# Two of six block inversions done over 16-token blocks, with their joins on TensorE, and a new order of the first batch

## The chip, the cores and the metric

The kernel runs on one core of a Trainium2 chip, in float32 throughout. The metric is the device time of one execution in microseconds (us), the median of several runs. Five engines have queues of their own and work through them in order: TensorE (PE, matrix products; its weight loads are listed apart as PEld), VectorE (DVE), ScalarE (ACT), GpSimd (POOL) and SyncE (SP), which here only issues transfers. TensorE writes to PSUM, eight banks of 128x512 float32; the other engines copy from there to SBUF.

## What is computed

The first half is a delta-rule attention over 4 batches, 8 heads, 768 tokens and head width 48; the second half mixes the result with a two-dimensional Fourier transform and a two-layer network:

```python
for t in range(S):                                    # per batch and head, state D x D
    y[t] = q[t] @ state
    state = state + beta[t] * outer(k_n[t], v[t] - state.T @ k_n[t])
u  = x + real(fft(fft(x, axis=1), axis=2))            # x: y as (batch, 768, 384)
un = (u - mean(u)) / sqrt(var(u) + 1e-6)
out = u + relu(un @ w_ch1) @ w_ch2                    # 384 -> 1536 -> 384
```

`k_n` is `k` over its norm. The two weight matrices come as float64 and are turned into float32 on the core.

## The kernel before

**Tiling of the attention.** Tokens are handled in chunks of 64. A *group* (index `g`, 24 in all, 6 per batch, `NL` = 6) is 128 tokens, two chunks, of all 8 heads. Within a chunk the recurrence becomes a triangular system: with G the products of the keys among themselves, the inverse of a unit lower triangular matrix is needed for each head and chunk. The kernel inverts blocks of 32 tokens (`W` = 32) and joins two of them to a chunk of 64 by two small products (in `pre_m`). Four groups make a *round* (`RL` = 4, index `r`, 6 rounds): their 128 partitions x 32 blocks are inverted together.

**The parts of the work**, each a generator that stops at its `yield`s, so that a schedule can advance several of them in turn:

- `pre_a(g)`: transposes the keys (4 products with the identity, tile `one` from `C`), copies them to `KT` on ScalarE, then 32 products `KT` x `KT` into `pair`, copied out to `G` (what is inverted) and `GX` (what joins two blocks). It also issues the load of a later group's keys into the buffer just read (`load_c(g + 3)`; three buffers `C`).
- `invert(r)`: all on VectorE: a transposition of the 1024 columns (L304), some 14 small operations for the norms, then forward substitution in 31 steps of two operations (L345 multiply into `tmp`, L349 add into `M`), and two transpositions (L352, L353). 
- `pre_q(g)`: the same for the queries: `QT`, and `LQ`, the masked products of keys and queries.
- `pre_m(g)`: scales the values (POOL L398), spreads the inverses (POOL L402), joins the two 32-blocks with two sets of 16 products and the copies L415 and L426, and makes `WT` and `U0` with 32 products.
- `step(g, c)`: the recurrence proper, one chunk: products S x WT, subtraction from U (L462), products U x K, addition to S (L481); after the second chunk of a group the outputs: S x QT and U x LQ into `pair`, copied and added (L502, L511) into `x`.
- `fourier(b)`: three folds of `x` (POOL L528 and L529, then six VectorE operations L532 to L539, each fold of token blocks t and t + 3), products with the tables `evt` and `odt` (`pf`), copies to `F`, and per 128 tokens the products with `dtab` (`pb`), additions and the statistics for the normalization.
- `mlp(b)`: three times 19 pieces: transposes of the normalized rows, 12 pieces of first-layer products (`ph`, into `hT`), 6 pieces of second-layer products (`po`).
- `weights()`: float64 to float32 in 12 pieces, six of w_ch1 and six of w_ch2, each a chain ScalarE (L231), VectorE (L232, L234, L237), ScalarE (L239), VectorE (L241, L243), POOL (L246). A piece uses the scratch of the piece before it, so one piece ends before the next is written. The pieces of w_ch2 use a scratch (tag `O`) that `fourier(0)` uses too.

**The order.** Inside `with tc.manual_schedule(...)` the order is written out by hand: first the keys of rounds 0 and 1, the inversions `inv0` and `inv1` in alternation on VectorE, the queries of batch 0, then `pre_m(0)` and the twelve steps of batch 0, with pieces of `inv1`, of the weights and of the folds put between them. After the block, batches 1 to 3 are interleaved: while the steps of batch b + 1 run, `mlp(b)` is spread beside them by `beside(n)`, with the keys and the inversion of the next round. There a scheduler places the instructions, and it also moves work from behind the block into gaps of it.

**What waits for what**, as far as the change touches it: `pre_m(g)` needs the round's inverse; `step(g, 0)` needs `pre_m(g)`; the folds need all six groups of a batch; `pf` needs the folds; the w_ch2 conversion needs `pf` to be done with its scratch; `po` needs w_ch2; `pre_m(8)` needs the inverse of round 2. Transfers that SyncE issues wait in SyncE's order for their buffers to come free. All PSUM tiles share pools of two buffers (`one`, `pair`, and `post` for everything after the attention).

## Time and profile before

| | us |
|---|---|
| three runs | 822.41, 826.55, 833.77 (median 826.55) |
| the profiled execution | 822.35 |
| its span, first to last instruction | 820.4 |
| first transposition of round 0's inversion starts | 15.64 |
| first product that reads round 0's inverse | 61.78 |
| first U x K product (`step(0, 0)`) | 69.27 |
| output of batch 0's last group added (L511) | 153.48 |
| last fold of batch 0 ends | 161.3 |
| last `pf` product of batch 0 ends | 174.2 |
| last weight piece: POOL starts | 236.32 |
| first product that reads round 2's inverse | 261.10 |

Busy times over the span: PE 706.0 (86%), VectorE 410.9 (50%), ScalarE 203.9, POOL 132.0. A profile line of a group reads: source line, engine, operation, output tile <- input tiles, shapes, count | busy us, mean ns of one | idle us just before them, and what ended that idle time. A line of the timeline reads: start, duration, engine, the same names, and in brackets the idle time before it. A float32 product appears as two records, so 32 products are `x64`; a transposition is one record. "PEclk" is the TensorE clock granted by its throttle, in tenths of full speed. Nearly all products are issued by one helper, so they all carry line L104 (L107 for transposes) and are told apart by their tiles.

### The profile page before, as it was taken

How to read it: one execution, taken by the hardware profiler on the slowest of the kernel's cores; microseconds unless marked ns; L12 is line 12 of the kernel's file. 1: busy time of each engine (PE TensorE's matmuls, PEld its weight loads, DVE VectorE, ACT ScalarE, POOL GpSimd, SP SyncE). 2: the span in 40 equal slices, each digit the busy share in tenths (PEclk: the TensorE clock that was granted, in tenths of full speed). 3: DMA queues.
4: the chain of work that ended last, by engine and by line, in shares of the span. 5: the costliest groups of instructions: out<-in, count | busy, mean ns of one | idle time of the engine just before them, and what ended most of it. 6: DMA issues, size and time to landing. Idle time of an engine off the chain costs nothing.

```text
span 820.4 us, 23216 instructions
## 1 busy us (share of the span) xinstructions
PE 706.0 (86%) x10344; PEld 543.3 (66%) x10344; DVE 410.9 (50%) x1004; ACT 203.9 (25%) x470; POOL 132.0 (16%) x150
## 2 busy tenths in 40 slices
PE   6537565398888999899998998899999999899998
PEld 4427464387656867568866767777768677686774
DVE  2897756546997118946258515698222141511110
ACT  4312333163321322124321223212223111210010
POOL 6231135302311101131100102102000020100000
PEclk8555555596998899999998999999999999899999
DMA  9821134323300321112121122002010000000000
GB/s 133 209 44 29 29 106 110 92 41 88 112 16 21 61 54 33 35 30 40 37 46 30 21 46 46 12 10 45 16 46 17 11 12 1 19 1 20 10 10 19
DMA packets 107382, 36.06 MB, mean 44 GB/s; under 512 B 99633, under 2 KB 102930, under 8 KB 107282
## 3 DMA queue, kind: packets, MB, share of 16 engines
q1 hardware_dynamic: 105586, 33.50, 18.3%
q8 instruction: 81, 1.33, 0.7%
q0 software_dynamic: 512, 0.79, 0.6%
q10 hardware_dynamic: 1184, 0.30, 0.3%
q14 instruction: 19, 0.16, 0.1%
HBM read 29.84 MB, written 4.72 MB: 42 GB/s over the span
## 4 chain that ended last, share of the span: by engine, by line
PE 55%; DVE 28%; issue 5%; POOL 5%; DMA 3%; ACT 3%; SPq 1%; ACTq 0%; POOLq 0%; DVEq 0%
PE po L104 17%; PE ph L104 17%; PE pair L104 8%; DVE M L349 5%; DVE tmp L345 5%; PE one L104 5%; PE pf L104 3%; DMA C<-in_k_dram 3%; PE one L107 2%; PE pb L104 2%; POOL w L246 1%; DVE A L304 1%; DVE A L352 1%; DVE G L353 1%; PE ptr L107 1%
## 5 line engine op out<-in xcount | busy, mean ns | idle before, releaser
L104 PE MATMUL ph<-unT,w 128*128 128x256 f32 x864 | 211.1, 399 | 9.5 <-DVE hT L619 5.9
L104 PE MATMUL po<-w,hT 128*128 128x384 f32 x576 | 198.1, 496 | 5.9 <-POOL w L246 3.2
L104 PEld LDWEIGHTS ph<-unT,w 128*128 128x128 f32 x864 | 166.0, 198 | 37.8 <-DVE hT L619 8.8
L104 PEld LDWEIGHTS po<-w,hT 128*128 128x128 f32 x576 | 108.4, 193 | 74.1 <-POOL w L246 3.3
L619 DVE TENSOR_SCALAR hT<-ph 128x256 f32<-128x256 f32 x72 | 30.3, 421 | 112.6 <-PE ph L104 112.6
L349 DVE TENSOR_TENSOR M<-M,tmp 128x135 f32<-128x135 f32 (+15 forms) x186 | 70.8, 382 | 4.8
L345 DVE TENSOR_TENSOR tmp<-A,M 128x60 f32<-128x60 f32 (+15 forms) x186 | 67.4, 364 | 4.4
L617 ACT ACTIVATE hT<-ph 128x256 f32<-128x256 f32 x72 | 27.5, 382 | 145.6 <-PE ph L104 142.5
L629 DVE TENSOR_TENSOR x<-x,po 128x384 f32<-128x384 f32 x24 | 13.2, 552 | 97.4 <-PE po L104 97.4
L104 PE MATMUL one<-V,MT 64*64 64x48 f32 x768 | 48.6, 245 | 0.9 <-ACT MT L426 0.8
L402 POOL TENSOR_TENSOR MT<-A,pack 128x512 f32<-128x512 f32 x24 | 26.1, 1096 | 136.2 <-PE one L104 85.3
L104 PEld LDWEIGHTS one<-V,MT 64*64 64x64 f32 x768 | 44.3, 163 | 2.8 <-ACT MT L426 1.7
L398 POOL TENSOR_TENSOR V<-V,nT 128x384 f32<-128x384 f32 x24 | 20.7, 863 | 154.5 <-DMA V<-in_v_dram 90.8
L104 PE MATMUL pair<-MT,K 64*64 64x64 f32 x768 | 43.5, 260 | 1.6 <-ACT MT L426 1.0
L104 PEld LDWEIGHTS pair<-MT,K 64*64 64x64 f32 x768 | 39.4, 154 | 3.5 <-issue 2.1
L104 PE MATMUL pair<-S,WT 48*64 48x48 f32 x704 | 22.9, 247 | 21.8 <-DVE S L481 17.5
L104 PEld LDWEIGHTS pair<-S,WT 48*64 48x64 f32 x704 | 17.1, 153 | 31.2 <-DVE S L481 18.6
L104 PEld LDWEIGHTS pair<-U,K 64*64 64x64 f32 x704 | 17.1, 153 | 29.1 <-DVE U L462 14.3
L104 PE MATMUL pair<-U,K 64*64 64x48 f32 x704 | 23.5, 248 | 14.4 <-DVE U L462 12.6
L104 PE MATMUL one<-G,GX 32*32 32x32 f32 x768 | 19.8, 207 | 14.9 <-DVE G L353 14.9
L481 DVE TENSOR_TENSOR S<-S,pair 128x192 f32<-128x192 f32 x40 | 14.0, 350 | 37.0 <-PE pair L104 36.9
L415 ACT ACTIVATE XM<-one 32x256 f32<-32x256 f32 x48 | 18.0, 375 | 54.9 <-PE one L104 53.8
(111 smaller groups left out, 928.6 us busy)
## 6 DMA issues: line engine op xcount, KB each, us to landing
w<-in_moe_w_ch_dram SPq DMA_DIRECT2D x12, 768.0 KB
Q<-in_q_dram SPq DMA_DIRECT2D x24, 192.0 KB
out_dram<-x SPq DMA_DIRECT2D x24, 192.0 KB
C<-in_k_dram SPq DMA_DIRECT2D x23, 192.0 KB
K<-in_k_dram SPq DMA_DIRECT2D x88, 48.0 KB
V<-in_v_dram SPq DMA_DIRECT2D x88, 48.0 KB
evt<-k_even SPq DMA_DIRECT2D x1, 579.0 KB
odt<-k_odd SPq DMA_DIRECT2D x1, 576.0 KB
```

The source lines that it names most:

```text
L104: nc.tensor.matmul(o, lhsT=lhsT, rhs=rhs, start=start, stop=stop, skip_group_check=True)
L107: nc.tensor.matmul(o, lhsT=src, rhs=ident[0:src.shape[0], 0:src.shape[0]], is_transpose=True, start=start, stop=True, skip_group_check=True)
L246: nc.gpsimd.tensor_tensor(dst, man.rearrange("p (c f) -> p c f", c=c), num.bitcast(F32).rearrange("p (c f) -> p c f", c=c), op=ALU.mult)
L345: nc.vector.tensor_tensor(t, A[:, j + 1:W, j:j + 1].broadcast_to([128, n, j + 1]), M[:, j:j + 1, 0:j + 1].broadcast_to([128, n, j + 1]), o ...
L349: nc.vector.tensor_tensor(M[:, j + 1:W, 0:j + 1], M[:, j + 1:W, 0:j + 1], t, op=ALU.add)
L398: nc.gpsimd.tensor_tensor(V.rearrange("p c j d -> p (c j) d"), V.rearrange("p c j d -> p (c j) d"), nT[:, m8, None].broadcast_to([128, 8, ...
L402: nc.gpsimd.tensor_tensor(MT, MTd[:, m8, None, :].broadcast_to([128, 8, 2, W]), m_blk[:, None, :, None].broadcast_to([128, 8, 2, W]), op=A ...
L415: nc.scalar.activation(XM[rw].rearrange("p m s -> p (m s)"), px[rw, 0:8 * W], ACT.Copy, scale=-1.0)
L481: nc.vector.tensor_tensor(s1v, s0.rearrange("p h j e -> p h (j e)"), pk, op=ALU.add)
L617: nc.scalar.activation(hT[:, fc, :], ph, ACT.Relu)
L619: nc.vector.tensor_scalar(hT[:, fc, :], ph, 0.0, None, op0=ALU.max)
L629: nc.vector.tensor_tensor(x[:, T, :], x[:, T, :], po, op=ALU.add)
```

## The change

1. **Rounds 0 and 1 are inverted by a new `invert16`** over blocks of 16 tokens: the substitution has 15 steps instead of 31, on both halves of a 32-block at once. A copy of G (`Gc`) is kept by POOL. Round 0 is inverted in one go, then round 1; before, they alternated. Rounds 2 to 5 keep `invert`.
2. **A new `join(g)`** for the eight groups of these rounds puts the 16-blocks together: 32 products `Gc` x `Md`, a scaled copy `Y`, 64 products of 16 columns, two VectorE additions.
3. **Loads.** The two query buffers hold keys at first, so that five key loads are issued at once; the loads of K and V on POOL's queue come after the first inversion has begun, `load_kv` in the steps one group earlier.
4. **Unread products** (`spin(n)`: n products of zero tiles, 128x128x128) stand at the head of TensorE's queue (18), between the queries' products (3 or 4 at a time), and two in each group of batch 0.
5. **The order of batch 0** is written anew: `join` and `pre_m` are advanced two or three groups ahead, a group's outputs come behind the next group's first products, queries 4 and 5 are prepared inside the first two groups, and the weights of w_ch1 fill slots after `inv1`.
6. **The third fold of batch 0** is done by VectorE instead of POOL, and the first two thirds of the first `pf` products are issued ahead of it.
7. **The stretch after it** (second layer's weight conversion, first 13 pieces of `mlp(0)`, the `pb` part of `fourier(0)`) is now inside the hand-written block. The third round's inversion and the first queries of batch 1 stand after its end.
8. The square-root table is loaded at the start, by a one-column operation.

In the diff, `fill()` advances `inv1` by four parts, and once that has ended the weights by one or two; `p2` is `pre_m(g + 2)`, `jn` holds `join(g + 3)`, and `conv` and `first` are the weights' pieces.

```diff
+    def home(g):
+        return Cs[g] if g < 3 else Qs[g - 3] if g < 5 else Cs[(g - 5) % 3]
...
 def pre_a(g):
-        K = Cs[g % 3]
+        K = home(g)
...
-        load_c(g + 3)
+        if g < 3:
+            load_c(g + 5)
+        elif g < 5:
+            load_q(g - 3)
+        else:
+            load_c(g + 3)
...
+    def invert16(r):
...
+        nc.gpsimd.memset(M2, 0.0)
+        nc.gpsimd.tensor_copy(Gc[0][:, r], G)
+        yield
+        nc.vector.transpose(A, G.rearrange("p m s -> p s m"))
+        yield
...
+        for j in range(V16 - 1):
+            n = V16 - 1 - j
+            t = wk.tile([128, 256], F32, tag="tmp", bufs=2, name="tmp")
+            t = t[:, 0:2 * n * (j + 1)].rearrange("p (e a b) -> p e a b", e=2, a=n)
+            sh = [128, 2, n, j + 1]
+            nc.vector.tensor_tensor(t, Ad[:, :, j + 1:V16, j:j + 1].broadcast_to(sh),
+                                    Md[:, :, j:j + 1, 0:j + 1].broadcast_to(sh), op=ALU.mult)
+            yield
+            nc.vector.tensor_tensor(Md[:, :, j + 1:V16, 0:j + 1], Md[:, :, j + 1:V16, 0:j + 1], t,
+                                    op=ALU.add)
+            yield
+        nc.vector.transpose(G.rearrange("p m s -> p s m"), M.rearrange("p t s -> p s t"))
+        nc.vector.transpose(A.rearrange("p m t -> p t m"), M)
+        nT = wk.tile([128, W], F32, tag="nT", bufs=2, name="nT")
+        nc.vector.transpose(nT, nrm)
+        rounds[r] = (A, G, nT)
+        yield
+
+    def join(g):
+        r, li = divmod(g, RL)
+        MTd, Md, _ = rounds[r]
+        py = ps_one()
+        for m in range(8):
+            for q4 in range(4):
+                rw = slice(W * q4, W * q4 + V16)
+                mm(py[W * q4:W * q4 + W, W * m:W * m + W], Gc[0][rw, r, 8 * li + m, :],
+                   Md[rw, 8 * li + m, :], m == 0)
+        Y = wk.tile([128, 8, W], F32, tag="QT", bufs=2, name="Y")
+        nc.scalar.activation(Y.rearrange("p m s -> p (m s)"), py[:, 0:8 * W], ACT.Copy,
+                             scale=m_upper)
+        yield
+        pm = ps_one()
+        for m in range(8):
+            for q4 in range(4):
+                rw = slice(W * q4, W * q4 + W)
+                mm(pm[rw, V16 * m:V16 * m + V16], Y[rw, m, :], MTd[rw, 8 * li + m, V16:W], m == 0)
+                o = 8 * V16 + V16 * m
+                mm(pm[rw, o:o + V16], MTd[rw, 8 * li + m, :], Y[rw, m, 0:V16], False)
+        for t, s0, o in ((Md, 0, 8 * V16), (MTd, V16, 0)):
+            d = t[:, 8 * li:8 * li + 8, s0:s0 + V16]
+            nc.vector.tensor_tensor(d, d, pm[:, o:o + 8 * V16].rearrange("p (m s) -> p m s", s=V16),
+                                    op=ALU.add)
+        yield
...
 def fourier(b):
+        early = b == 0
         for t in range(TH):
+            if early and t == TH - 1:
+                for par, tab, n, _ in tabs:
+                    sums(0, par, tab, n, range(t))
+                yield
+            fold = nc.vector if early and t == TH - 1 else nc.gpsimd
...
 with tc.manual_schedule(engines=engines):
+        unread.append(ps_post([128, 512], "unread"))
+        spin(18)
...
+        for g in range(2 * RL):
+            if g == RING:
+                drain(qs[0])
+            advance(keys[g])
+            if g > 0:
+                advance(keys[g - 1])
+            if g == RL:
+                advance(inv0, 3)
+                load_kv(0, nc.gpsimd)
+                load_beta(1)
+        drain(keys[-1])
+        advance(inv1)
+        load_kv(1, nc.gpsimd)
+        drain(inv0)
...
+        for qg in qs[1:4]:
+            spin(3)
+            advance(qg)
+            spin(3)
+            drain(qg)
+        spin(4)
+        js = [join(g) for g in range(2 * RL)]
+        pms = [pre_m(g) for g in range(NL)]
+        advance(js[0])
+        advance(js[1])
+        advance(inv1)
+        spin(2)
...
+        for g in range(NL):
+            s0, s1 = step(g, 0), step(g, 1)
...
+            if g > 0:
+                advance(s0)
+                fill()
+                advance(out_g)
...
+            advance(p2)                # pre_m(g + 2)
+            advance(s0)
+            fill()
...
+            for jg in jn:
+                advance(jg)
+            if g in (0, 1):
+                advance(qs[g + 4])
+            spin(2)
+            advance(s1)
+            fill()
+            advance(p2)
...
+        drain(first)
+        advance(conv)
+        advance(f, 2)
+        side, done = mlp(0), 0
+        advance(side)
+        for _ in range(4):
+            advance(f)
+            advance(side)
+            advance(conv, 3)
+            advance(side)
+            advance(conv, 3)
+            done += 2
...
+        drain(conv)
+        inv = invert(2)
+        advance(inv)
```

## The prediction

> **What bounds the kernel now.** I read the busy tenths first: they show which engine leads in which stretch.
>
> ```profile
> PE   6537565398888999899998998899999999899998
> ...
> DVE  2897756546997118946258515698222141511110
> ...
> PEclk8555555596998899999998999999999999899999
> ```
>
> A slice is 20.5 us. From the tenth on TensorE is busy nine tenths and more; in the first eight it is half idle, its clock at 0.5, and VectorE leads. The end is thus set by a chain through batch 0 (about 160 us) and then by TensorE's work. The change touches the first part, and the timeline gives its marks:
>
> ```profile
> 15.64 1.94 DVE L304 STREAM_TRANSPOSE A<-G 128x1024 f32<-128x1024 f32 x1 [15.64 <-ACT G L291]
> ...
> 69.27 0.68 PE L104 MATMUL pair<-U,K 64*64 64x48 f32 x16 [0.88 <-ACT U L444]
> ...
> 153.48 0.55 DVE L511 TENSOR_TENSOR x<-x,pair 128x384 f32<-128x384 f32 x1
> ...
> 236.32 1.86 POOL L246 TENSOR_TENSOR w<-wtmp 128x768 f32<-128x768 f32 x1 [5.90 <-DVE wtmp L243]
> ...
> 261.10 1.07 PE L104 MATMUL one<-G,GX 32*32 32x32 f32 x32 [2.26 <-DVE G L353]
> ```
>
> These are the start of round 0's inversion, the first step, the last output of batch 0, the last weight piece, and a product that waits for round 2's inverse. After the last TensorE has hardly a gap. So I carry each mark forward, and what 261.10 becomes moves the end.
>
> Two things decide the rates. The costliest VectorE groups are the substitution's:
>
> ```profile
> L349 DVE TENSOR_TENSOR M<-M,tmp 128x135 f32<-128x135 f32 (+15 forms) x186 | 70.8, 382 | 4.8
> L345 DVE TENSOR_TENSOR tmp<-A,M 128x60 f32<-128x60 f32 (+15 forms) x186 | 67.4, 364 | 4.4
> ```
>
> And the clock, by single stretches of 3.4 us (span, TensorE busy, granted clock):
>
> ```profile
> 8.15:11.56 3.41, 3.41 (x101) 1.00 1.39 168
> ...
> 118.50:121.90 3.40, 3.40 (x106) 0.50 0.27 66
> ...
> 414.30:417.70 3.40, 2.71 (x144) 1.00 0.19 36
> 185.60:189.00 3.40, 2.21 (x39) 1.00 0.54 197
> ```
>
> The granted clock changes at 11.6, 15.0, 154.9, 158.2, 165.1, 189.2 and 202.7 us, on a grid of 3.41 us. The first row's 1.00 is no full speed yet: 64 KT records take 1.18 us in it, 51 take 0.74 us at 14.45, that is 18 and 14 ns each. The second row is full of small products and stays at half. The third has small products alone, once the clock is up, and keeps it; the fourth, with 1.2 us idle, loses it. So small products keep a clock more easily than they raise it.
>
> **Up to the first inversion.** 18 unread products are 36 records. A 193-column `pf` record takes 0.35 us at half clock, a 97-column `pb` record 0.14 at full; for 128 columns I estimate 0.25 and 0.14. Begun at 1.2, at half clock for one grid period, they end near 8. Before, TensorE's first transposes ran at 4.54 but waited for loads; now five key loads have landed by 8 (before, 170 GB/s were shared with POOL's K and V loads, now moved back). Then five transposes (0.66) and four KT sets (0.86) at full clock are 6.7, the copies 0.8: 15.6, as before. Gain nothing; at half clock +4. The square-root table's load (1.28 at 15.90) was hidden by the transposition at 15.64: nothing.
>
> **Round 0's inversion.** Transposition and root 2.3; the small operations took 4.6 from 17.90, less one transposition (0.24) and half of the wide multiply (0.6): 3.8. Substitution: 15 steps of two operations, 1360 elements in sum. Rows: 31 elements 0.20, 60 0.22, 112 0.28, 135 0.30, so 0.17 + 0.00095 each: 7.7, with 30 gaps of 0.033 8.7. The forms have one more dimension than any row; 10% for that is 0.9. POOL beside it costs: at 25.73 an `M` operation took 1.29 instead of 0.32 while POOL ran L387; POOL now also copies G and issues eight loads (0.65 each) there: 2.5. Three transpositions 3.8. Sum 21.1: done at 36.7, against 61.5. `inv1` is no longer between, and comes later.
>
> **What is late next.** Queries 1 to 3 stand ahead of the joins in TensorE's queue, and query 3's load stands on SP behind two 768 KB weight loads and the tables. From 19 us on 3.9 MB are ahead of it; the stretch 20.5 to 41 moved 209 GB/s, its first half about 250: landed at 34.5, then transposes, unread products and QT x KT: the joins begin at 40, not 37. If it lands when the last such query did before (43.7), +9.
>
> **Joins and `pre_m`.** A join is 64 + 128 records. The trace has none of 16 columns. Fastest row: KT, eight tile positions, 13.4 ns at full clock; slowest: G,GX, two positions, 0.69 for 32, 21.6 ns. Joins use four positions; I take the KT rate, since these are the smaller products: 2.6 us each, the other end is 4.1. The Trainium skill, "TensorE: Matmul & The Clock Gate", Part 1, says that starts never come closer than about 25 ns, however few the columns; per record that makes a join 4.8 us, eight of them 18 us more, and would eat the gain. The KT row has 13.4 ns per record and 27 per product, so it agrees only if a product counts once; I go by the row. Up to the first step: three joins 7.7, four parts of `pre_m` 2.8, its products 1.9, unread 0.6, waits 1.5, copies 1.1: 15.6. First step at 55.6, against 69.27.
>
> **Batch 0's steps.** Group 0 is held by the rest of `inv1` on VectorE (substitution, 3.8 of transpositions) to 67.5. Per later group TensorE has at full clock: steps 3.1, `pre_m` 3.3, join 2.6, unread 0.6, a query 1.3 (group 1). VectorE's weight pieces add waits: a piece's chain is 7.1 (0.6 + 1.0 + 0.6 + 0.9 + 0.6 + 1.0 + 1.9, gaps 0.5), two thirds of it in VectorE's queue, ahead of U and S. Groups 1, 2, 3 (two joins) take 10.2, 9.2, 12, group 4's chain 6.6: last S of group 4 at 105.5 (before 137.8). The folds stay in the step's way: 3.3 of VectorE before group 5's first U, then a weight part, POOL's sums (2.3) and 3.3 more before its S, 16 `pf` records 4.5, outputs, and the third fold on VectorE 3.7 (before 7.3 with POOL's wait behind L246): 26.5, before 23.5. Folds end at 132, `pf` (11.5) at 143.5, before 174.2. The early K and V loads cost SP nothing; POOL waited 90.8 us for V before.
>
> **Where gain goes back.** Before, the w_ch2 pieces started in VectorE's queue right after `pf`, spread over 64 us (174.2 to 238.2) while TensorE ran batch 1's first steps and `po`. Now the first piece stands behind two `pb` groups, statistics and the first `ph`: 13.5 later. Then six pieces of 7.1, and between them `pb` additions (2.2 each), hT and the normalizations, 6 not hidden: 48.6. Done at 205.6. Only then comes round 2's inversion, which before ran beside the pieces from 176.5: transposition 2, small operations 4.6, substitution 24, transpositions 3.8, other VectorE work between 5.2: 39.6. So 261.10 becomes 245.2, after `pf` 101.7 instead of 86.9. In TensorE's order 48 first-layer products stand ahead of that mark, before 59: 11 x 0.53 = 5.8 us of work still to do. Without this stretch's cover for the inversion the 30.7 won at `pf` are 10.1 at the end.
>
> **Sum.** 820.4 - (261.1 - 245.2) + 5.8 = 810.3, a gain of 10.1. The profiled execution took 822.35, the median is 826.55; off the middle of both, 824.4, that is **814**. Break-even: `pf` ending at 153.6 instead of 143.5. A measurement tells some 2% from no change, here 16.5.
>
> **Rivals.**
> 1. *Slower: the clock falls in batch 0.* At half clock the joins and `pre_m` take 18 instead of 13, groups 1 to 3 16.6, 14.4 and 17.8. `pf` then ends near 167, past 153.6: 13.4 lost, 838. For it: the full row at 118.5 that stays at 0.5, and query 3's wait, over 5 us idle just before the joins. Against it: the row at 414.3, and that the unread products and KT sets raised or would raise the clock. 0.17.
> 2. *Joins at the slow rate*, 21.6 ns: 192 x 8 x 8.2 ns = 12.6 more, the gain is spent: 827. For it: four positions lie between two and eight. 0.13.
> 3. *The stretch after `pf` holds nothing back*: the `pb` additions fit into the chain's waits (6 less), and round 2's inverse is not what TensorE waits for (3 to 4): 804, and less if query 3 lands early (up to 4). 0.2.
>
> Forecast 0.5, 805 to 823. The range reaches over rivals 2 and 3 to the middle of the first and query 3's late end: 799 to 838. Faster by over 2% (under 810): a third of the forecast and nearly all of rival 3, 0.36. Slower (over 843): the first rival with slow joins or the late query, 0.08. The rest 0.56.
>
> **What would show it.** First U x K at 55 to 57 and a clock near 1 from there to 100; `pf` of batch 0 ending near 143; a gap on TensorE of some 7 us before round 2's inverse is read, near 245; join records at 13 to 15 ns. Wrong if the clock row stays at 5 in the third to sixth slice, if the joins wait for query 3 past 45, or if TensorE has no gap after the weights.

## The result, and the profile after

The changed kernel is **slower**: 853.56 us median of four runs (849.72 to 858.21), against 827.77 for the kernel before, a ratio of 1.0312 with a 95% interval of 1.0218 to 1.0406. Forecast were 814 us and a range of 799 to 838: wrong in sign and out of the range. The profiled execution took 850.89 us, its span is 849.1 (before 822.35 and 820.4).

The page of the changed kernel, TensorE, VectorE and clock by slices of 21.2 us:

```profile
PE   7658888666579899979998999889999999999998
...
DVE  1816444535579611992628812499412131421110
PEclk9665555597689999999999999999999999989999
```

VectorE's 9, 7 and 7 in slices 3 to 5 have become 1, 6 and 4, as meant; TensorE is busier (8 in slices 4 to 7, where it had 7, 5, 6 and 5), and its clock is still 5 in slices 4 to 8. The prediction named a 5 in slices 3 to 6 as a sign that it is wrong; slice 3 has a 6, the others have it. Its two other signs came too: the joins waited for query 3 past 45 (47.03 below), and TensorE has hardly a gap behind the weights (0.66 below, forecast some 7).

The marks, from the timeline (start, duration, operation, and in brackets the idle time before it and what ended it):

```profile
17.03 1.98 DVE L409 STREAM_TRANSPOSE A<-G 128x1024 f32<-128x1024 f32 x1 [16.04 <-ACT G L318]
...
47.03 1.09 PE L109 MATMUL one<-pack,Q 128*128 128x128 f32 x4 [9.42 <-DMA Q<-in_q_dram]
...
56.71 0.29 DVE L485 TENSOR_TENSOR G<-G,one 128x128 f32<-128x128 f32 x1 [17.15 <-PE one L106]
...
74.60 0.68 PE L106 MATMUL pair<-U,K 64*64 64x48 f32 x16
...
169.59 0.55 DVE L643 TENSOR_TENSOR x<-x,pair 128x384 f32<-128x384 f32 x1 [3.06 <-ACT x L634]
...
246.31 1.82 POOL L268 TENSOR_TENSOR w<-wtmp 128x768 f32<-128x768 f32 x1 [5.16 <-DVE wtmp L265]
...
287.97 0.69 PE L106 MATMUL one<-G,GX 32*32 32x32 f32 x32 [0.66 <-DVE G L380]
```

Start of the inversion, query 3's transposition, the first addition of a join, the first step, the last output of batch 0, the last weight piece, and the product that reads round 2's inverse. Before, the five that the prediction showed stood at 15.64, 69.27, 153.48, 236.32 and 261.10.

The substitution's groups hold two rounds less, as they should (124 instead of 186):

```profile
L372 DVE TENSOR_TENSOR tmp<-A,M 128x31 f32<-128x31 f32 (+15 forms) x124 | 44.6, 359 | 3.5
...
L376 DVE TENSOR_TENSOR M<-M,tmp 128x31 f32<-128x31 f32 (+15 forms) x124 | 43.6, 352 | 3.3
```

The same four stages of both kernels: up to `pf`'s end, to the end of the second weights' conversion, to the product that reads round 2's inverse, to the end. The columns are span, then busy time and records of TensorE, its weight loads, VectorE, ScalarE and POOL, then the granted clock. Before:

```profile
0.00:174.20 174.20, 100.40 (x2507) 86.01 (x2507) 109.46 (x235) 54.91 (x112) 56.53 (x67) 0.58 0.43 92
174.20:238.20 64.00, 54.73 (x665) 41.78 (x665) 53.09 (x121) 24.65 (x49) 16.89 (x14) 0.87 0.26 70
238.20:261.10 22.90, 20.38 (x217) 14.87 (x215) 21.76 (x56) 2.51 (x6) 1.71 (x2) 1.00 0.10 27
261.10:820.40 559.30, 530.53 (x6962) 400.67 (x6962) 226.57 (x594) 121.78 (x303) 56.89 (x68) 0.97 0.12 27
```

After:

```profile
0.00:184.10 184.10, 136.42 (x4148) 122.47 (x4148) 82.24 (x190) 57.20 (x120) 49.92 (x64) 0.63 0.41 88
184.10:248.10 64.00, 38.97 (x262) 30.31 (x262) 37.47 (x77) 17.95 (x34) 14.49 (x13) 0.76 0.18 54
248.10:288.00 39.90, 35.91 (x540) 24.62 (x540) 37.52 (x96) 8.51 (x20) 7.33 (x9) 0.96 0.20 42
288.00:849.10 561.10, 531.71 (x7042) 402.05 (x7042) 227.88 (x598) 122.51 (x305) 56.96 (x68) 0.98 0.12 27
```

So the 28.7 us more of span are 9.9 up to the end of `pf`, 17.0 up to round 2's inverse, and 1.8 behind it. Forecast were -30.7, +14.8 and +5.8. VectorE's 27 us of saved work did come; TensorE has 1641 records and 36 us of busy time more in the first stage. What it waited for there, in the waits up to 185 us (total, times, longest):

```profile
PE pair L106 <- issue: 10.4, 6, 2.2
PE one L109 <- DMA Q<-in_q_dram: 9.4, 1, 9.4
PE one L106 <- issue: 8.9, 7, 2.3
```

"issue" is idle time for which the profile shows no wait at all. The kernel before has 2.0 us of it before 200 us, this one 19.4.

In some runs TensorE's clock is half for 14 to 17 us between 550 and 600 us, and the span behind everything told here is then 4 to 12 us longer, so I compare experiments by the end of batch 0's `pf` (before 174.2, after 184.2) and give each one's median with the ratio to the kernel before and its 95% interval. The end of `pf` comes from one profiled execution each; two of the same code up to there, the changed kernel and e12, have it at 184.2 and 183.8.

### The profile page after: what moved, and what is told of

It reads as the page before. It is cut to its first block, busy times and chain, and to the rows that moved or that the text cites. A ratio compares the mean times of both kernels' runs of the same rounds, so it can differ in the third digit from the quotient of the medians.

```text
span 849.1 us, 26492 instructions
## 1 busy us (share of the span) xinstructions
PE 743.0 (88%) x11988; PEld 579.4 (68%) x11988; DVE 385.1 (45%) x959; ACT 206.2 (24%) x478; POOL 128.7 (15%) x151
## 3 DMA queue, kind: packets, MB, share of 16 engines
q1 hardware_dynamic: 105586, 33.50, 17.8%
q8 instruction: 94, 1.54, 0.8%
## 4 chain that ended last, share of the span: by engine, by line
PE 60%; DVE 24%; issue 5%; POOL 4%; ACT 4%; DMA 2%; SPq 0%; POOLq 0%; DVEq 0%; ACTq 0%
PE ph L106 17%; PE po L106 16%; PE pair L106 10%; PE one L106 8%; DVE M L376 5%; DVE tmp L372 5%; PE pf L106 3%; PE one L109 3%; PE unread L197 2%; DMA Q<-in_q_dram 2%; POOL w L268 1%; PE pb L106 1%; PE ptr L109 1%; DVE A L379 1%; POOL E L680 1%
## 5 line engine op out<-in xcount | busy, mean ns | idle before, releaser
L106 PE MATMUL ph<-unT,w 128*128 128x256 f32 x864 | 219.3, 408 | 26.5 <-DVE x L725 11.8
L106 PEld LDWEIGHTS ph<-unT,w 128*128 128x128 f32 x864 | 170.2, 203 | 58.0 <-ACT Q L720 9.8
L106 PE MATMUL one<-V,MT 64*64 64x48 f32 x768 | 46.1, 238 | 1.2 <-issue 0.7
L372 DVE TENSOR_TENSOR tmp<-A,M 128x31 f32<-128x31 f32 (+15 forms) x124 | 44.6, 359 | 3.5
L376 DVE TENSOR_TENSOR M<-M,tmp 128x31 f32<-128x31 f32 (+15 forms) x124 | 43.6, 352 | 3.3
L106 PEld LDWEIGHTS pb<-dtab,F 97*128 97x128 f32 (+1 forms) x192 | 26.9, 211 | 6.5 <-DVE x L774 2.7
L106 PE MATMUL pb<-dtab,F 97*128 97x97 f32 (+1 forms) x192 | 28.8, 300 | 2.9 <-DVE x L774 2.3
L558 ACT ACTIVATE MT<-one 32x256 f32<-32x256 f32 x48 | 17.9, 373 | 52.0 <-PE one L106 44.3
L106 PE MATMUL pair<-KT 48*32 48x64 f32 x1536 | 22.3, 236 | 8.6 <-issue 5.3
L594 DVE TENSOR_TENSOR U<-U,pair 128x192 f32<-128x192 f32 x44 | 15.4, 351 | 30.5 <-PE pair L106 27.8
```

The lines of the kernel that those rows point to most:

```text
L106: nc.tensor.matmul(o, lhsT=lhsT, rhs=rhs, start=start, stop=stop, skip_group_check=True)
L372: nc.vector.tensor_tensor(t, A[:, j + 1:W, j:j + 1].broadcast_to([128, n, j + 1]), M[:, j:j + 1, 0:j + 1].broadcast_to([128, n, j + 1]), o ...
L376: nc.vector.tensor_tensor(M[:, j + 1:W, 0:j + 1], M[:, j + 1:W, 0:j + 1], t, op=ALU.add)
L558: nc.scalar.activation(MT[rw, :, 1, :], py[rw, 0:8 * W].rearrange("p (m s) -> p m s", s=W), ACT.Copy)
L594: nc.vector.tensor_tensor(U.rearrange("p (jj jp) e -> p jp jj e", jp=2), U.rearrange("p (jj jp) e -> p jp jj e", jp=2), pw[:, :, 0:2 * D]. ...
```

## The experiments

My theory now: **F**, TensorE runs out of instructions in the dense streams of short products that the joins brought, and these gaps and thin products keep its clock at half. Rivals: **Q**, the late query alone; **D**, the joins' data chain or VectorE; **C**, the clock by itself.

**e1, the queries first.** The block with `weights()` and the loads of `evt`, `odt` and `dtab` is moved behind the loop over queries 1 to 3.

```
-        side = weights(); advance(side); dma evt, odt, dtab
         for qg in qs[1:4]: ...
         spin(4)
+        side = weights(); advance(side); dma evt, odt, dtab
```

> The two first weight loads, the cosine tables and dtab are issued on SP behind the loads of queries 2 to 5 instead of ahead of them. Theory Q (the late query is one of the costs, and it shifts everything behind it): TensorE's 9.42 us wait for query 3 is under 2 us, the joins begin at 42 to 43 instead of 51.8, the last S of group 4 and the end of pf come 8 to 10 us earlier (149.4 and 184.1 in the changed kernel), profiled execution 841 to 843 against 850.9. Theory F (idle 'issue' and the half clock set the pace of batch 0, and the wait only moves): the joins begin earlier, but the stalls behind them and the steps at half clock remain as long, and since VectorE must still run round 1's substitution, pf ends 4 to 10 us earlier. Both give a gain; a pf end that moves less than 3 us would say that the query was no cost at all. If the clock is kept up by the missing gap, groups 1 to 3 would shrink from 18.7, 14.2 and 19.7 us towards 10, 9 and 12, and pf would end near 150.

`pf` ended at 173.6 instead of 184.2, the joins began at 40.2, the span is 839.3, the median 846.37 (1.0273, 1.0195 to 1.0351). Q holds: a cost of 10.6 us, and not the only one. Nothing else moved: idle "issue" stayed at 20.2 us.

**e2, no joins.** `join` yields twice and does nothing.

> The eight joins are left out: their 1536 TensorE records, eight ScalarE copies and sixteen VectorE additions. The inverses of rounds 0 and 1 then consist of the 16-token diagonal blocks alone. Theory F (the dense streams of short products outrun TensorE's supply of instructions, which shows as idle 'issue', 14 us in 52 to 145 us, and these gaps keep the clock at half): idle 'issue' of TensorE before 185 us falls from 19.4 us to under 7, and pf of batch 0 ends 30 us earlier or more (near 150), the profiled execution 820 to 825. Theory P (a join costs only its own products): 8 joins of 2.2 to 2.8 us at half clock, 20 us less at most, with the clock row still at 5 in the slices from 60 to 160 us: pf end near 164 and 830. Theory D (VectorE and the fixed order set the pace): less than 10 us earlier.

`pf` ended at 156.8, 27.4 us earlier: 3.4 us for each join. Idle "issue" fell to 8.0 us. Ahead of the folds the clock came up for three short stretches only, 51 to 61, 98.5 to 102 and 122.5 to 126. Median 829.72 (1.0045, 1.0001 to 1.0089). That lies between F (150) and P (164): the stalls went, as F says, but most of the half clock stayed, as P says.

**e3, no unread products.** `spin` does nothing.

> All unread products are left out (54 products, 108 records; 18 of them at the start). Theory K (they keep the clock up where it is up): without them the clock is half from 15 us on without a break, the key sets and round 0's inverse come 2 to 4 us later, the first U x K later still, 853 to 858. Theory W (they only take TensorE's time: two of them 0.53 to 1.06 us at half clock in each of six groups, and 3 to 4 us between the queries): pf of batch 0 ends 4 to 8 us earlier and the profiled execution takes 843 to 847. Theory N (they lie in waits): within 2 us.

`pf` at 181.8 instead of 184.2; median 853.85 (1.0348, 1.0276 to 1.0419). The clock is then half from 25 to 165 without a break, but neither K's loss nor W's 4 to 8 us follow: nearest to N.

**e4, the end as before.** Everything behind the folds as in the kernel before.

```
-        advance(conv); advance(f, 2); side, done = mlp(0), 0 ... drain(conv)
-        inv = invert(2); advance(inv); drain(pre_q(NL)); pm = pre_m(NL) ...
+        drain(f)
+        inv = invert(2)
...
+        if b == 0: run([(part(side, 13), 1), (conv, 3)]); done = 13
```

> Only the stretch behind the folds is put back: pf, pb, statistics, the first layer's first pieces, the second weights' conversion and round 2's inversion run as in the kernel before, beside each other; everything up to the folds stays changed. My prediction's step (this stretch gives back about 20 us: 14.8 up to round 2's inverse and 5.8 behind it): from the end of pf 86.9 us to the product that reads round 2's inverse and 559.3 more, so a span near 830 and a profiled execution of 830 to 834, against 850.9. Rival (the stretch costs nothing, TensorE has the same work in any order and the loss lies wholly in front of pf): 847 to 852.

From the end of `pf` (182.3) to the read of round 2's inverse (271.7) it took 89.4 us, against 103.8: 14.4 us of loss lie in that stretch. Median 839.81 (1.0173, 1.0107 to 1.0239), 14 us below the changed kernel.

**e5 and e6, the joins' records without joins.** In e5 each join is 96 unread products of 32 x 32 on 16 columns, in e6 five of 128 x 128 on 128 columns; neither reads or writes anything of the kernel.

```
 def join(g):
-    ...
+    short(32); yield; short(64); yield      # e5: 192 records, as in a join
+    spin(2); yield; spin(3); yield          # e6: 10 records
```

> In place of each join stand 96 unread products of zeros, 32 x 32 on 16 columns, at the same four row positions (32 where the join's first part stood, 64 where its second did): as many TensorE records as in the joins (192 each), but no operand and no result that anything waits for. The joins' part of rounds 0 and 1 is left out of the inverse. Theory F (it is the number of instructions: TensorE runs out of them): idle 'issue' before 200 us is back at 16 to 20 us (19.4 with joins, 8.0 without) and pf ends at 178 to 184 (184.2 with, 156.8 without). Theory D (the stall hides a wait for the join's data, its copy or its additions): idle 'issue' stays at 7 to 10 and pf ends at 170 to 175, 8 x 2 us behind the kernel without joins.

> In place of each join stand five unread products of 128 x 128 on 128 columns (two and three), ten records that take as long at half clock as a join's 192 (2.65 us), a twentieth of its instructions. The joins' part of rounds 0 and 1 is left out of the inverse. Theory F: idle 'issue' before 200 us stays at 7 to 9 us as without joins, and pf ends near 156.8 + 21 = 178 if the clock stays at half, that is 6 us ahead of the changed kernel. Theory C (the half clock is what sets the pace of batch 0, and long products can raise it, which short ones do not): the clock is at 1 in more of 60 to 160 us than without joins (there 98 to 102 and 122 to 126 only), and pf ends at 150 to 165 in spite of the added work. Under D idle 'issue' falls too, but so it would in the kernel with short products.

The waits of TensorE up to 185 us, e5:

```profile
PE one L109 <- DMA Q<-in_q_dram: 12.4, 1, 12.4
PE pair L106 <- issue: 8.9, 6, 3.1
PE unread L467 <- issue: 8.0, 5, 2.2
```

e6, whose "issue" is no longer among the first:

```profile
PE one L109 <- DMA Q<-in_q_dram: 8.9, 1, 8.9
PE ptr L109 <- DVE un L728: 5.4, 1, 5.4
PE pair L106 <- DVE pair L604: 4.5, 1, 4.5
PE pair L106 <- ACT x L614: 4.4, 2, 2.9
```

With short products that nothing waits for, `pf` ended at **185.1**, the span is 850.6 and idle "issue" 18.8 us: the changed kernel again, without its joins. So D falls: the joins' data, copies and additions are not the price, the short products themselves are. With long ones it ended at **155.5**, with 4.4 us of "issue", even a little before the kernel with none (one execution each).

This doesn't yet say that the number of instructions is the whole price, for the clock differs too: from 60 to 135 us it is at full for 24 us in e6, 8 in e2, 4 in e5 and none in the changed kernel, so the long products did not take as long as was planned. Up to `pf`, e5 has 28.8 us more of TensorE's busy time than e2 (136.3 against 107.5), 10.8 us more of "issue" and 11.2 less of its other waits; e6 has 8.3 us more busy time and 3.6 less "issue". Short products cost in two ways, then: they take the array's time at half clock, and TensorE waits for instructions.

**e7, e1 and e4 together.**

> The queries' loads ahead of the weights and tables, and the stretch behind the folds as before, together. If the two losses add up: pf ends at 172 to 174, round 2's inverse is read 89 us later, and the rest is 560: span 821 to 824, profiled execution 823 to 826, the same as the kernel before within 2%. If they cover each other (the same idle time counted twice): 830 to 837, as with the end alone.

Span 821.9, `pf` at 173.5, round 2's inverse read at 264.7: the losses add up. Median 829.36 (1.0011, 0.9949 to 1.0073): level with the kernel before. So the slowdown is these two parts; what is left of the change, new inversion and order of the first rounds, gains nothing.

**e8 and e10, round 1 whole.** On e7, round 1 by the old substitution without joins, `fill` taking 6 parts of it; e10 also issues its first transposition behind round 0's inversion.

```
-        inv0, inv1 = invert16(0), invert16(1)
+        inv0, inv1 = invert16(0), invert(1)
...
-        js = [join(g) for g in range(2 * RL)]
+        js = [join(g) for g in range(RL)]
```

> As the kernel with the queries first and the end as before, but round 1 is inverted by the whole substitution on VectorE (31 steps, no joins), spread over the first two groups; joins are left for round 0 alone. A join costs TensorE 27.4 / 8 = 3.4 us with its stalls, four of them 13.7; the substitution adds some 16 us to VectorE, which waits for TensorE 37 us before 185 us. Theory J (the joins of round 1 are the cost and VectorE has the room): pf ends 10 to 14 us earlier, at 159 to 163, span 808 to 813, profiled execution 810 to 816: 1 to 1.5% faster than the kernel before. Theory V (VectorE's substitution stands in front of the steps' U and S, as it did in the kernel before): 0 to 5 us earlier or later, 820 to 830.

> The queries first, the end as before, round 1 by the whole substitution without joins, and round 1's first transposition issued behind round 0's inversion instead of ahead of it (ahead of it, it held VectorE's queue until 28.2 us and round 0's inverse came at 47.5 instead of 35.3). Theory J (four joins less are worth 3.4 us each, and VectorE has the room for the 31 steps): round 0's inverse at 35 to 36, pf ends at 160 to 164, span 808 to 813 against 821.9. Theory V (VectorE's steps of round 1 hold up the steps of batch 0): pf ends at 170 to 176, span 819 to 826.

e8: `pf` at 175.5, median 828.81 (1.0025, 0.9965 to 1.0086). The edit had a fault of its own: the transposition stood in VectorE's queue ahead of round 0's inversion and waited for the last keys until 28.23, so that round 0's came 12 us later. e10, without it: 169.3 and 819.87 (0.9958, 0.9912 to 1.0004). Behind the second group (group 1) each join less saved some 3.5 us, as J says (groups 2 and 3 with their one and two joins: 14.7 and 19.1 us in e7, 10.6 and 12.6 in e10), but the second group's last addition to S came 8 us later than in e7, as V says.

**e9 and e11, more unread products** in e7 and in e10: three at four places ahead of the first step, four or six more in each group (46 in all).

> The queries first and the end as before, and more unread products of 128 x 128: three at each of four places between the first joins and the first step, and two at three more places in every group (eight a group instead of two; 42 more in all, 0.53 us each at half clock, 0.27 at full). Theory C (what raises or holds the clock is the array work of a 3.41 us window, each record's columns weighted by the share of the rows and columns that it uses; in the ten profiles so far 97% of the windows are told by a bound near 1330 such columns, which the groups with 600 to 1000 miss): the added work brings the windows over the bound, the clock is at 1 in most of 60 to 150 us, groups 1 to 3 take 12 to 14 us instead of 14 to 19, pf ends at 155 to 165 instead of 173.5, span 805 to 813 against 821.9. Theory F (instructions set the pace, whatever the clock): the clock may rise, but the groups take 14 us and more, pf ends at 170 to 180, span 818 to 828. If the clock stays at half the 42 products cost up to 22 us: pf end near 190.

> Both: round 1 whole behind round 0's inversion, and the added unread products. If the half clock and the joins' instructions are two costs that add up: pf ends 5 to 10 us earlier than with either alone, at 150 to 156, span 798 to 805, 2 to 3% faster than the kernel before. If VectorE's chain (inversion, weight pieces, U and S) is what is late once TensorE is quick: no earlier than the better of the two.

`pf` ended at 186.2 and 178.5, 12.7 and 9.2 us later than without; medians 842.05 (1.0194, 1.0095 to 1.0292) and 829.26 (1.0057, 1.0018 to 1.0096). In e9 the clock stayed at half from 74 to 135, and the windows there hold no more than 1280 weighted columns (see the last section): the added work did not reach the bound. In e11, with four joins, it did at times: the clock is at full for 31 of the 90 us from 60 to 150, where e10 has none, and yet TensorE is busy 9.3 us longer up to `pf`. So unread products cost here what they take, or more than the clock that they raise gives back; what full clock by itself would be worth stays open.

**e12, a burst alone,** behind the last product of the changed kernel.

```
+    for i in range(24):  matmul 128 x 128 on 128 columns, unread
+    for i in range(512): matmul 32 x 32 on 16 columns, rows 32 * (i % 4), unread
```

> The changed kernel with a burst behind its last product: 24 unread products of 128 x 128 on 128 columns (about 6.5 us at full clock), then 512 unread products of 32 x 32 on 16 columns at four row positions (1024 records, 2048 instructions with the weight loads), nothing else running. Only these are read. Theory F: the first one or two hundred records run at 10 to 17 ns each, then TensorE waits for instructions after every 128 or so: 1024 records in 25 us or more, a mean over 24 ns. Rival (the engine can do 10 to 17 ns per record for as long as it likes; the stalls in batch 0 came from the traffic of loads): 11 to 18 us without idle time over 0.3 us. By theory C the clock falls to half one window after the burst's begin, although TensorE is never idle by the rival.

The timeline of its end:

```profile
845.76 5.08 PE L999 MATMUL last<-pack 128*128 128x128 f32 x44
850.77 1.48 PE L1003 MATMUL last<-pack 32*32 32x16 f32 x154
854.12 1.25 PE L1003 MATMUL last<-pack 32*32 32x16 f32 x128 [1.87 <-issue]
857.59 1.90 PE L1003 MATMUL last<-pack 32*32 32x16 f32 x128 [2.22 <-issue]
861.33 1.90 PE L1003 MATMUL last<-pack 32*32 32x16 f32 x128 [1.84 <-issue]
864.80 1.91 PE L1003 MATMUL last<-pack 32*32 32x16 f32 x128 [1.57 <-issue]
868.27 1.90 PE L1003 MATMUL last<-pack 32*32 32x16 f32 x128 [1.56 <-issue]
871.74 1.91 PE L1003 MATMUL last<-pack 32*32 32x16 f32 x128 [1.57 <-issue]
875.49 1.57 PE L1003 MATMUL last<-pack 32*32 32x16 f32 x102 [1.84 <-issue]
```

With nothing else running, TensorE does 154 short records at once, then exactly 128, pauses, 128, pauses. Six blocks from 854.12 to 875.49 are 21.37 us for 768 records, **27.8 ns per record**, though 128 of them take 1.25 us (9.8 ns each) at full and 1.90 at half clock. A faster clock shortens the block and lengthens the pause, so in such a stream the clock does not set the pace: F holds, the rival doesn't.

**e13 to e15, fewer records.** e13: e7 with both rounds whole, no joins. e14: e10 with `drain(inv1)` moved from the second group to the third's begin (e13 has this too). e15: e7, where the second set of a join's products, which gives the transposed block of the first, is replaced by a transposition on VectorE.

```
-                mm(pm[rw, o:o + V16], MTd[rw, 8 * li + m, :], Y[rw, m, 0:V16], False)
...
+        nc.vector.transpose(Md[:, m8, :].rearrange("p m s -> p (m s)"),
+                            MTd[:, m8, :].rearrange("p m s -> p (m s)"))
```

> The queries first, the end as before, and both rounds by the whole substitution, one after the other, in the changed order; no joins, 1536 records less; round 1 may take VectorE until the third group. Theory S (the shorter substitution doesn't pay for its joins): round 0's inverse comes 15 to 16 us later, at 51 to 53, but its three joins (13.5 us from the joins' begin to the last additions) are gone: first U x K at 58 to 64, as with joins, and the five later joins' 3.4 us each are saved: pf ends at 156 to 164 against 173.5, span 804 to 812. Rival (round 0's late inverse is on the path in full, and VectorE's two substitutions hold up the first groups as they did in the kernel before): pf ends at 168 to 176, span 816 to 825.

> As the kernel with round 1 whole behind round 0's inversion, but round 1's rest is forced out at the third group's begin instead of in the middle of the second. Theory L (the forced end made the second group 8 us longer than with joins): second group's S at 90 to 93 instead of 97.4, pf ends at 162 to 166 instead of 169.3, span 810 to 814. Rival (VectorE has that work to do before the third group anyway): pf within 2 us of 169.3.

> The queries first, the end as before, and in every join the second set of 32 products, which yields the transposed block of the first, is replaced by one transposition of 128 x 256 on VectorE behind the addition (one addition less): 128 records instead of 192, 512 less in all, with the same result. Theory F (records have a price of 17 us per 1000 at least, 27.8 as in the burst): pf ends 9 to 14 us earlier, at 160 to 165 against 173.5, span 808 to 813. Rival (the price is per join, its three waits from TensorE to ScalarE to TensorE to VectorE, not per record): less than 4 us earlier, span 818 to 824.

e15 ended `pf` at 163.3, 10.2 us before e7, for 512 records: 20 ns each. What it costs VectorE, per join, beside an addition saved:

```profile
46.48 0.29 DVE L483 TENSOR_TENSOR A<-A,one 128x128 f32<-128x128 f32 x1 [2.09 <-PE one L106]
46.80 0.45 DVE L485 STREAM_TRANSPOSE G<-A 128x256 f32<-128x256 f32 x1
```

Median 819.35 (0.9896, 0.9817 to 0.9974). All eight joins and their waits are still there, so the price goes by records, not by joins. It has both parts again: up to `pf` the joins' records keep TensorE busy for 15.3 us instead of 23.5, and "issue" is 13.7 instead of 17.9. e14: 163.6 and 818.44 (0.9907, 0.9870 to 0.9943), 5.7 us before e10: the forced end was the fault. e13: 166.2 and 817.94 (0.9898, 0.9839 to 0.9956), between theory and rival: its first step begins at 64.4, where e7 with joins has it at 63.4. With joins of 192 records the shorter substitution is worth 1.0 us to the first step. e13 has no 16-token inversion at all and is still 1% faster than the kernel before: that much is worth what is left of the change, its order and loads above all.

**e16 and e17, what helped, together:** queries first, end as before, round 1 whole as in e14, round 0's joins as in e15; e17 without the two unread products in each group.

> Everything that helped, together: queries first, end as before, round 1 by the whole substitution spread to the third group, and round 0's four joins with 128 records and a transposition. If records go on costing 20 us per 1000 (256 less than with round 1 whole): pf ends at 157 to 160 against 163.6, span 806 to 813, 1.5 to 2% faster than the kernel before. Rival (without round 1's joins something else is late in the groups, VectorE's substitution): pf at 162 to 164 and no more than 1% faster.

> The same without the two unread products of each of the six groups; those ahead of the steps stay. The clock is at half in the groups with them and without them, so they hold nothing up, and two take 1.06 us of TensorE there. Theory W (they are only a cost): pf ends 3 to 6 us earlier than in the kernel with them. Rival (they lie in TensorE's waits for U and S): within 2 us.

`pf` ended at 156.8 and 156.1. e16: 812.46 (0.9838, 0.9774 to 0.9902); e17: **807.36, 0.9771 (0.9717 to 0.9824)**, the best of all, 2.3% faster than the kernel before (1.8 to 2.8%). At `pf` the two are level, as the rival of e17 says; their intervals overlap, so whether the products cost anything is not settled. The stages of e17:

```profile
0.00:156.10 156.10, 113.39 (x3112) 100.69 (x3120) 98.64 (x214) 54.95 (x116) 53.11 (x67) 0.64 0.49 103
156.10:246.20 90.10, 78.23 (x880) 59.36 (x879) 77.10 (x176) 27.42 (x55) 19.45 (x17) 0.87 0.21 57
246.20:804.70 558.50, 529.10 (x6962) 399.03 (x6962) 226.08 (x594) 121.91 (x303) 56.16 (x68) 0.97 0.13 27
```

A thousand records less than the changed kernel in the first stage, and 28 us less of it.

## Why the prediction was wrong, step by step

**Right.** Up to the inversion 17.03 (forecast 15.6); round 0's inverse at 37.8 (36.7). Behind `pf`: first weight piece 14.4 after it (13.5), the conversion 49.5 (48.6), round 2's inverse read 39.9 later (39.6); in all 103.8 (101.7). From the last addition to S of group 4 to the end of `pf` it took 34.8 (38.0). One reading was off and cost nothing: from the tenth slice on TensorE is busy eight tenths and more, not nine. The sum for round 0's inverse came so near with an error of its own: its terms add up to 22.0, not 21.1, which makes 37.6. Less right was where TensorE would wait: not 7 us before that inverse (0.66), but beside the weights, where it is idle 25.0 of 64 us (9.3 before). That the changed end costs was a right step: 16.9 + 1.8 us by the marks, 20.6 forecast.

**Wrong: all between 38 and 149 us.** `pf`'s end came 40.7 us after its forecast. The terms:

1. *Query 3 lands at 34.5.* It landed at 47.0. I had summed the bytes ahead of it and left out when it can start: there are two query buffers, so it waits until query 1 is transposed (30.66 to 31.7), and SP began to issue it at 31.75. Behind the weights and tables the issue alone took 6.37 us, against 0.37 in e1, where they come later and it began at 31.01; whether SP's issue or the bytes on their way made it late is not told apart. I had named +9 as the other end; e1 measured 10.6.
2. *A join at the KT rate, 13.4 ns per record, 2.6 us.* Measured: 27.4 us for eight (e2), 17.8 ns per record, where the sum had put 18 on the path (7.7 ahead of the first step, 2.6, 2.6 and 5.2 in groups 1 to 3). The row that I took it from is one of 64 records, half a block of the burst; no row of such length can show a limit that acts every 128. The rule that I weighed and set aside, that starts come no closer than about 25 ns (the Trainium skill, "TensorE: Matmul & The Clock Gate", Part 1), does not hold for single records here, which start 9.8 ns apart (19.6 per product). That its number is near the mean of 27.8 in a long stream may be chance.
3. *Steps and `pre_m` at full clock.* My first rival said the clock would fall and priced it at 23.5 us (`pf` near 167; the terms that it names add up to 22.4). It did fall, from 58 to 167. Groups 1 to 3, each from its first S x WT product to the next group's, took 19.3, 14.2 and 19.7 us; the rival had 16.6, 14.4 and 17.8, the forecast 10.2, 9.2 and 12. Without joins (e2) they still took 40.3 us together instead of 21. Terms 1 and 2 leave 40.7 - 10.6 - 9.3 = 20.8 for this one, by subtraction only.

The step that failed most is thus the clock, taken as full in the steps of batch 0; I had weighed the other case and given it 0.17. By the sum's own break-even (`pf` at 153.6), this term alone (143.5 + 20.8 = 164.3) makes the change slower, the query alone (154.1) barely so, the joins alone (152.8) not quite.

The second and third are tied. The three groups in the changed kernel (span, TensorE's busy time and records, clock, then share of the DMA engines and GB/s):

```profile
87.90:107.10 19.20, 14.97 (x474) 0.50 0.34 77
107.10:121.30 14.20, 13.23 (x461) 0.50 0.33 83
121.30:141.00 19.70, 16.18 (x650) 0.50 0.31 73
```

At the burst's 27.8 ns the 461 records of group 2 need 12.8 of its 14.2 us, the 650 of group 3 need 18.1 of 19.7. By this estimate a full clock could not have made them much shorter. But TensorE is busy for 44.4 of the 53.1 us, and idle "issue" takes only 4.7 of them, none in group 2: what held these groups up was mostly short products on an array at half clock, and a thin stream of small products cannot raise the clock (see the last section). That the joins' records cause the loss is shown (e2, e5, e15). How it divides between the supply of instructions and the half clock is not, since no run kept the clock up through the groups with all their joins.

The price of the first 18 unread products was right (they end at 8.0, forecast near 8), their use was not: without any of them `pf` ends 2.4 us earlier.

## What to carry to other kernels

Before moving work to TensorE as many small products, count records as well as columns: each thousand of them cost 18 to 20 us here (e2, e15), since they ran at half clock and long streams of them went at the pace at which instructions arrive. No short row of a profile shows that pace, so look for "issue" and measure a burst. For a load, ask when its buffer comes free and what its queue has to issue ahead of it, not only how many bytes are ahead. Judge each part of a large change by itself: here the new order and the 16-token inversion of round 0, with a third of the join records left, were worth 2%, hidden under the late query and the changed end, which cost 10 and 14 us, and the rest of the joins' records.

## What the runs showed of the hardware

**Instructions arrive in blocks.** The profile's page counts 94 packets and 1.54 MB on the instruction queue of this kernel (81 and 1.33 MB before): 16 KB each, and 23976 TensorE instructions (records and weight loads) are 255 per packet, 20688 before likewise. The burst pauses after each 128 records, that is 256 instructions, one packet. The Trainium skill, "Runtime: NRT & Kernel Launch", "Instruction fetch mechanics", gives the same blocks of 256 and says that their fetch is mostly hidden; here it is not: 1.56 to 2.22 us of idle time per block, a block each 3.6 us. The idle "issue" in batch 0 has the same step: its twelve pauses of over 0.4 us in the changed kernel (19.1 of the 19.4 us) come ahead of the 222nd, 349th, 604th, 986th, 1114th, 1241st record and so on. Most of them are whole blocks of 127 or 128 records apart, and counted in blocks of 128 all twelve lie within 17 places. e5, where unread products stand for the joins, has twelve pauses at such places too, and the one long pause of the kernel before comes ahead of its 222nd record too. So these pauses belong to places in the stream of instructions and not to what the products there compute; that the wait is for the packet is inferred from this and from the counts.

**The clock goes by array work, not by busy time.** Full windows of 3.4 us at half clock that stay there, in the changed kernel (span, busy, records, clock, then DMA share and GB/s):

```profile
95.40:98.80 3.40, 3.40 (x72) 0.50 0.45 82
129.60:133.00 3.40, 3.40 (x82) 0.50 0.72 195
```

And the burst, which loses full clock:

```profile
850.00:853.40 3.40, 2.24 (x162) 1.00 0.02 5
853.40:856.80 3.40, 1.25 (x128) 0.94 0.02 5
856.80:860.20 3.40, 1.90 (x128) 0.50 0.02 5
```

I weighted each record's columns with the share of the 128 rows and 128 columns of the array that it uses (a 128 x 128 record on 128 columns counts 128, a 64 x 64 on 48 counts 12, a join's 1) and summed them over the clock's own windows of 3.413 us, 4580 in the 19 profiled executions. A sum of 1334 or more is followed by full clock, less by half, in 97.6% of them, with one bound for both states (94% of the windows at half, 99% of those at full): under 1000 in 9 of 737, over 1500 in 3393 of 3418. The best bound on busy time tells 86%; of 431 windows at half clock with TensorE busy at least 95%, 224 raised it. At 128 records to a window a record has to count 10.4 on average, which a stream of joins cannot. The bound is fitted to these runs; none was made to test it but e9 and e11, and they are among the 19.
